# A fused attention and gated-unit kernel: a cap on the loads in flight, a different first quad, fewer paddings and another written-out order

## The chip, the cores and the metric

The kernel runs on one core of a Trainium2 chip. A core has five engines that run side by side, each with its own stream of instructions: TensorE (PE in the profile, with its weight loads as PEld), VectorE (DVE), ScalarE (ACT), GpSimd (POOL) and SyncE (SP), which here only issues DMAs. They wait for each other through semaphores. SBUF is the on-chip memory of 128 partitions; PSUM is the memory of eight banks (called B0 to B7 here) that PE writes. The metric is device time in microseconds (us) of one execution.

## The reference

Eight batches of eight heads, 576 positions, head size 64. Attention is causal by blocks of 64 positions; its output, heads side by side, is x with 512 columns. A gate is a causal convolution over five positions with one weight per tap and column, put through a sigmoid; the output is (gate * (x @ w_val)) @ w_out. Inputs and output are float32.

```python
block_i, block_j = pos[:, None] // 64, pos[None, :] // 64
scores = where(block_i >= block_j, q @ k.T / 8, -1e9)
attn = softmax(scores) @ v                        # (8, 8, 576, 64)
x = attn.transpose(0, 2, 1, 3).reshape(8, 576, 512)
gate_pre[s] = sum(conv_w[k] * x[s - 4 + k] for k in range(5))
out = (sigmoid(gate_pre) * (x @ w_val)) @ w_out
```

## The kernel before, in words

The work is cut into words, and the order of all words is written out by hand in one string, PLAN (a few more in START). `run` goes through the string and records the instructions of each word; so each engine's stream has its instructions in the order of the words. A word is a name, its indices and, after an @, the engine (A, D, P for ACT, DVE, POOL) or the PSUM banks that it uses: `cq.1.0@P` casts tensor 0 (q; 1 is k) of quad 1 on POOL.

Attention runs over 16 quads of four heads, each with two pairs of heads (pair p belongs to quad p // 2).
- `Lqk` loads q or k of a quad (576 KB) on SP's queue into one of five float32 buffers (qks), `cq` casts it to two-byte floats (qk16, three buffers), `tq` transposes it on DVE into qT or kT (two of each). In the kernel before, the cast always puts two neighbouring positions side by side (j innermost), so that the transpose can move them as one four-byte element: 576 elements a partition.
- Head r of the quad lies on partitions 32r to 32r+31 (in two chunks c), so a score matmul uses 32 rows of PE's array, and matmuls of different r use different rows. `kz` copies k's first and last block into a small tile. `s.a.t` computes one of three parts t of the score matrix for all four heads; `s.a.t.h` only for the two heads of half h. Part t = 2 needs positions from 256 on alone.
- `e` is the exponential on ACT, PSUM to pt (two-byte, six buffers), 192 in all. `m` (mask, POOL) copies block 0 to the end of pt and zeroes the masked corners.
- `Lv`, `Lvt` load v of a pair (two DMAs of 128 KB) and the tails of a batch; `cv`, `cvt` cast them on POOL. A column of ones beside v gives the sum of the weights.
- `av.p.h` multiplies weights by v (15 matmuls), `n` divides by the sum on DVE, `xtr` transposes x on PE, and `xt` brings it back to SBUF (xt).

The gated unit works in 13 units of 288 or 384 positions. `cn` is the convolution on PE: 32x32 tiles with diagonal weights (DG), 80 matmuls for a unit, or 40 for a half (`cn.n.h`, two of the four row groups); `th` is the gate's tanh on ACT, `val` the product with w_val, `gv` their product on DVE, `o` the product with w_out, `oc` its copy to one of five buffers (osb) on ACT or DVE, `st` the store on SP's queue.

Memsets ahead of PLAN and the word `pm` in it fill what never changes: ones behind pt and zeros ahead of xt. `w` are matmuls on zeros; `cw`, `cT` and `DG` make the taps' diagonals.

Quad 0 is loaded in halves (`Lqh`, `cqh`, `tqh`): each partition's first ten and last eight positions, all four DMAs on SP's queue, the word `pm` standing between their casts and `kz.0` on POOL.

In the built program, each DMA on SP's queue waits for the landing of the eighth DMA before it; loads wait besides for the cast that frees their buffer, stores for their `oc`.

Of the kernel before, what the change touches and what calls it, by code (L numbers as in the profile page):

```python
# [10 lines left out]
Lqh.0.0 Lqh.1.1  # L11
# [3 lines left out]
Lqh.0.1 cqh.0.0@D tqh.0.0 Lqh.1.0 cqh.1.0@A Lcn cqh.1.1@D cqh.0.1@P w@0 w@0 w@0 w@0 cw@0 tqh.1.1  # L15
Lvt.0 tqh.0.1 tqh.1.0 pm kz.0@P s.0.1.0@12 s.0.2@5634 Lqk.1.1 cvt.0 e.0.1.0 e.0.1.1 e.0.2.3 cT
cq.1.1@P Lqk.1.0 s.0.0.1@70 s.0.1.1@12 Lv.1 e.0.2.2 e.0.1.3 tq.1.1 e.0.0.3 e.0.0.2 kz.1@D cq.1.0@P
s.0.0.0@34 DG cv.1 tq.1.0 e.0.1.2 Lqk.2.1 e.0.0.1 m.1 e.0.0.0 s.1.1.1@07 e.0.2.1 Lqk.2.0 s.1.0.1@12
e.0.2.0 e.1.0.3 e.1.0.2 Lv.0 av.1.0@3 cq.2.1@P av.1.1@4 e.1.1.3 n.1.0 s.1.1.0@56 Lv.3 n.1.1 m.0
e.1.1.2 s.1.2.1@31 cv.0 xtr.1@2 av.0.1@4 e.1.2.3 cq.2.0@P tq.2.1 e.1.2.2 cv.3 av.0.0@0 s.1.0.0@71  # L20
e.1.1.0 Lqk.3.0 Lqk.3.1 Lv.2 m.3 kz.2@D e.1.1.1 e.1.0.1 xt.1 tq.2.0 cq.3.0@P n.0.1 n.0.0 s.1.2.0@23
s.2.2.1@56 Lv.5 e.1.0.0 e.1.2.1 Lvt.1 av.3.0@4 av.3.1@1 Lv.4 s.2.1.1@70 e.1.2.0 s.2.0.1@23 n.3.0
e.2.2.3 cq.3.1@P n.3.1 e.2.2.2 xtr.0@4 tq.3.0 e.2.1.3 cv.2 xtr.3@1 xt.0 tq.3.1 e.2.1.2 s.2.0.0@56
m.2 xt.3 e.2.0.3 s.2.1.0@40 av.2.0@7 cv.5 e.2.0.2 kz.3@D Lqk.4.1 e.2.0.0 n.2.0 e.2.0.1 cvt.1
av.2.1@1 s.2.2.0@23 e.2.1.0 m.5 s.3.2.0@56 n.2.1 cv.4 av.5.0@7 e.2.1.1 e.2.2.0 e.2.2.1 xtr.2@1
av.5.1@0 n.5.0 s.3.1.0@42 Lwv.0 e.3.2.1 cq.4.1@P Lqk.4.0 e.3.2.0 s.3.0.0@37 e.3.1.0 s.3.1.1@56
e.3.1.1 e.3.1.2 n.5.1 xt.2 xtr.5@0 m.4 e.3.1.3 tq.4.1 kz.4@D e.3.0.1 cq.4.0@P e.3.0.0 Lwv.1 xt.5
av.4.1@1 Lv.7 av.4.0@2 n.4.0 n.4.1 s.3.0.1@40 e.3.0.3 s.3.2.1@56 Lqk.5.0 m.6 cn.0.0@23 tq.4.0
e.3.0.2 e.3.2.2 e.3.2.3 wv.1@D cn.1.0@71 th.1.1 th.1.0 wv.0@D s.4.0.0@04 cv.7 s.4.1.0@56 s.4.0.1@17
m.7 th.0.1 th.0.0 e.4.1.0 cq.5.0@P val.0.1@2 av.7.0@3 e.4.1.1 Lqk.5.1 val.1.1@5 e.4.0.2 Lvt.2  # L30
e.4.0.0 val.0.0@6 gv.0.1 n.7.0 cn.0.1@23 e.4.0.1 cq.5.1@P gv.1.1 gv.0.0 tq.5.1 s.4.2@4650 e.4.0.3
th.0.3 th.0.2 s.4.1.1@17 e.4.2.1 Lv.6 e.4.2.0 wv.2@D tq.5.0 val.1.0@2 e.4.1.2 Lqk.7.0 Lvt.3 av.7.1@3
cv.6 Lqk.6.0 av.6.0@4 e.4.1.3 wv.3@P m.8 e.4.2.2 gv.1.0 av.6.1@6 n.7.1 e.4.2.3 Lv.11 s.5.2.1@21
e.5.2.3 Lqk.6.1 n.6.0 cn.1.1@73 kz.5@P e.5.2.2 n.6.1 s.5.1@4056 th.1.2 cvt.3 th.1.3 Lv.8 Lwo.2
e.5.1.1 e.5.1.2 xtr.7@1 xtr.4@2 xtr.6@3 e.5.1.0 cv.11 val.0.2@7 Lv.9 xt.7 val.1.3@1 xt.4 s.5.2.0@20
xt.6 e.5.1.3 Lv.10 e.5.2.1 e.5.2.0 gv.1.3 s.5.0@3456 e.5.0.1 e.5.0.0 cvt.2 gv.0.2 val.1.2@1 gv.1.2
val.0.3@7 cn.3.0@02 cq.6.0@P gv.0.3 tq.6.0 e.5.0.2 cq.6.1@P cv.8 Lwo.1 cn.2@4713 tq.6.1 Lwo.0
e.5.0.3 th.2.3 th.2.2 th.3.1 th.3.0 val.2.2@5 th.2.0 cq.7.0@P th.2.1 av.8.1@6 gv.2.2 m.11 val.2.3@1
# [24 lines left out]
n.19.1 av.18.0@2 o.0.8@3 s.11.1@5047 xt.16 xt.17 oc.0.8@D e.11.1.2 n.18.0 m.20 Lvt.6 cv.21
s.11.0.1@16 o.1.0@3 e.11.1.3 xtr.19@2 val.6.2@4 e.11.1.0 e.11.0.3 cv.23 Lqk.13.1 val.5.1@7 xt.19
e.11.0.2 e.11.1.1 val.5.2@2 oc.1.0@A m.21 cq.13.0@P Lv.24 s.11.2@0516 tq.12.1 gv.5.1 cv.22 e.11.2.0
gv.6.2 e.11.2.1 s.11.0.0@37 e.11.2.2 e.11.2.3 kz.12@D av.21.0@4 gv.5.2 n.21.0 av.20.1@2 xtr.18@0
val.6.0@5 e.11.0.1 xt.18 av.20.0@4 av.21.1@1 e.11.0.0 n.20.1 s.12.2@6023 m.23 gv.6.0 cv.24 n.20.0
m.22 s.12.1.0@75 Lv.26 e.12.2.3 cq.13.1@P av.23.1@4 e.12.2.2 n.21.1 e.12.2.0 cq.14.0@P tq.13.0
# [32 lines left out]
def kernel(  # L101
# [70 lines left out]
    def f32(i):  # L172
        return BK[i][0:128]
# [11 lines left out]
    def half(h):  # L185
        return (slice(0, 5), slice(5, 9))[h]

    def load_half(i, h, m):
        load_qk(0, i, m, half(h))
# [28 lines left out]
    def cast_half(i, h, m):  # L218
        cast_qk(0, i, m, half(h))
# [256 lines left out]
```

## Time and profile before

| | us |
|---|---|
| median of three runs | 189.88 (189.83 to 193.27) |
| the profiled execution | 188.78 |
| its span, first to last instruction | 186.9 |
| PE busy | 168.9 |
| DVE busy | 131.7 |
| ACT busy | 130.0 |
| POOL busy | 104.3 |

The span is what the profile's views divide; the execution's own time is 1.9 us longer. Busy is the time in which an engine had an instruction under way. In a line of the page's second part each digit is one fortieth of the span (4.67 us) and gives a share in tenths, 9 being 90% or more. The mean granted clock of PE is 0.958. DMA moved 30.42 MB in and 9.44 MB out; its packets took 70.7% of the 16 DMA engines' time.

In a line of the timeline stand the start, the duration, the engine, the line of the kernel, the operation, out<-in, partitions x elements, a count, and in brackets the idle time of the engine before it with what ended it. Line 124 is the helper that records every matmul, and line 228 the one that records every copy, so there the names of the tiles tell the step.

### The profile page before, as it was taken

The numbers are of one execution on the slowest core, as the hardware profiler recorded it, in microseconds if no ns is written. First come the engines' busy times: TensorE is split into PE (matmuls) and PEld (weight loads), VectorE is DVE, ScalarE is ACT, GpSimd is POOL, SyncE is SP. The second block draws the span as 40 slices with busy tenths as digits, with TensorE's granted clock in tenths as the row PEclk, the third lists the DMA queues.
The fourth block names the chain that finished last, engine by engine and source line by source line (L and its number), as shares of the span: only waits on it lengthen the run. The fifth ranks groups of instructions, "written<-read, shape, count | busy, mean of one in ns | idle before, by whom it ended". The sixth has DMA issues, their size and how long they took to land.

```text
span 186.9 us, 8148 instructions
## 1 busy us (share of the span) xinstructions
PE 168.9 (90%) x3433; PEld 111.0 (59%) x3433; DVE 131.7 (70%) x289; ACT 130.0 (70%) x266; POOL 104.3 (56%) x205
## 2 busy tenths in 40 slices
PE   7635999999996899899999689999999999999991
PEld 2323767776775368456667458666666668654440
DVE  6743997968695579788975588966779677832730
ACT  3393899999998187689898467698779865042342
POOL 4898899599966638788466256929074312000000
PEclk9965799999999699999999999999999999999997
DMA  6999899966999789868987999707861023003685
GB/s 202 287 347 284 226 281 383 365 203 166 238 244 402 186 226 349 208 207 221 346 215 157 262 289 297 206 4 237 257 199 61 22 95 117 4 4 112 239 308 187
DMA packets 49407, 40.39 MB, mean 216 GB/s; under 512 B 39253, under 2 KB 39509, under 8 KB 49370
## 3 DMA queue, kind: packets, MB, share of 16 engines
q1 hardware_dynamic: 49226, 39.73, 70.7%
q8 instruction: 27, 0.44, 1.1%
q10 hardware_dynamic: 144, 0.13, 0.2%
q14 instruction: 10, 0.08, 0.1%
HBM read 30.42 MB, written 9.44 MB: 213 GB/s over the span
## 4 chain that ended last, share of the span: by engine, by line
PE 65%; DVE 16%; DMA 5%; issue 5%; POOL 3%; ACT 2%; SPq 0%; ACTq 0%; DVEq 0%; POOLq 0%
PE B L124 62%; DVE kT L243 4%; PE B L310 4%; DVE qT L243 4%; DMA out_dram<-osb 3%; DVE x L303 3%; DMA qks<-in_q_dram 2%; DVE rc L302 1%; DVE xt L316 1%; DVE gv L359 1%; ACT pt L274 1%; POOL qk L228 1%; POOL pt L420 1%; ACT th L348 1%; DVE osb L228 1%
## 5 line engine op out<-in xcount | busy, mean ns | idle before, releaser
L274 ACT ACTIVATE pt<-B 128x512 f16<-128x512 f32 x192 | 98.3, 620 | 19.1 <-PE B L124 16.6
L228 POOL CAST qk<-qks 128x1152 f16<-128x1152 f32 (+1 forms) x31 | 42.3, 1377 | 5.1 <-DMA qks<-in_q_dram 3.9
L124 PE MATMUL B<-qT,kT 32*128 32x448 f16 (+3 forms) x640 | 39.5, 296 | 5.5 <-DVE qT L243 4.0
L124 PE MATMUL B<-v,pt 128*128 128x65 f16 x896 | 35.9, 195 | 2.9 <-issue 2.5
L124 PE MATMUL B<-xt,w_val 128*128 128x384 f16 (+1 forms) x208 | 37.9, 316 | 0.2 <-issue 0.2
L124 PEld LDWEIGHTS <-pt 128*128 128x128 f16 x960 | 33.8, 99 | 7.0 <-issue 4.7
L124 PE MATMUL B<-w_out,gv 128*128 128x512 f16 (+1 forms) x148 | 35.8, 380 | 2.1 <-DVE osb L228 1.1
L359 DVE SCALAR_TENSOR_TENSOR gv<-th,B 128x384 f16<-128x384 f32 (+1 forms) x52 | 26.1, 518 | 11.8 <-PE B L124 11.3
L303 DVE TENSOR_TENSOR x<-B,rc 128x320 f16<-128x320 f32 x64 | 31.5, 492 | 2.5 <-DVE rc L302 0.2
L124 PEld LDWEIGHTS <-kT 32*128 32x128 f16 x640 | 18.1, 94 | 22.2 <-issue 9.2
L348 ACT ACTIVATE th<-B 128x384 f32<-128x384 f32 (+1 forms) x52 | 20.7, 482 | 13.0 <-PE B L124 7.7
L124 PEld LDWEIGHTS <-w_val 128*128 128x128 f16 x208 | 18.3, 98 | 9.7 <-issue 1.2
L280 POOL COPY pt<-pt 64x128 f16<-64x128 f16 x32 | 10.5, 328 | 22.9 <-ACT pt L274 20.0
L124 PEld LDWEIGHTS <-gv 128*128 128x128 f16 x148 | 13.7, 99 | 15.4 <-issue 3.1
L222 POOL CAST v<-vst 128x512 f16<-128x512 f32 x32 | 19.3, 613 | 5.9 <-DMA vst<-in_v_dram 2.8
L243 DVE STREAM_TRANSPOSE kT<-qk 128x576 f32<-128x576 f32 (+2 forms) x17 | 19.7, 1156 | 4.1 <-POOL qk L228 4.1
L228 ACT COPY osb<-B 128x512 f32<-128x512 f32 (+1 forms) x18 | 10.2, 571 | 16.3 <-PE B L124 15.8
L302 DVE RECIPROCAL rc<-B 128x5 f32<-128x5 f32 x64 | 12.0, 188 | 13.5 <-PE B L124 12.0
L228 DVE COPY osb<-B 128x512 f32<-128x512 f32 x19 | 13.1, 688 | 11.2 <-PE B L124 9.0
L243 DVE STREAM_TRANSPOSE qT<-qk 128x576 f32<-128x576 f32 (+2 forms) x17 | 19.7, 1156 | 0.7 <-PE B L124 0.6
L281 POOL MEMSET pt<- 64x384 f16 x32 | 13.2, 413 | 10.3 <-ACT pt L274 8.8
L316 DVE COPY xt<-B 128x576 f16<-128x576 f16 x32 | 14.1, 450 | 4.5 <-PE B L310 4.5
(42 smaller groups left out, 123.3 us busy)
## 6 DMA issues: line engine op xcount, KB each, us to landing
out_dram<-osb SPq DMA_DIRECT2D x35, 256.0 KB, 2.9
qks<-in_k_dram SPq DMA_DIRECT2D x15, 576.0 KB, 6.7
qks<-in_q_dram SPq DMA_DIRECT2D x15, 576.0 KB, 6.9
vst<-in_v_dram SPq DMA_DIRECT2D x64, 128.0 KB, 5.2
vtst<-in_v_dram SPq DMA_DIRECT2D x8, 128.0 KB, 6.4
w_st<-in_moe_w_val_dram SPq DMA_DIRECT2D x2, 512.0 KB, 6.3
w_st<-in_moe_w_out_dram SPq DMA_DIRECT2D x4, 256.0 KB, 5.1
qks<-in_q_dram SPq DMA_DIRECT2D x1, 320.0 KB, 3.0
```

What stands on the lines that cost most here:

```text
L124: nc.tensor.matmul(out=out, lhsT=lhsT, rhs=rhs, start=start, stop=stop, skip_group_check=True)
L222: nc.gpsimd.tensor_copy(out=v16s[p % NV][0:128, 0:4, 0:2, 0:64], in_=vst[p % NVS][0:128])
L228: (eng.copy if eng is nc.scalar else eng.tensor_copy)(out=o, in_=i)
L243: nc.vector.transpose(out=(qT, kT)[i][a % NQT][0:128].bitcast(fp32).rearrange("p c (x n) -> p c n x", n=9)[:, :, n], in_=qk16[(2 * a + i) ...
L274: nc.scalar.activation(out=pts[(2 * a + r // 2) % NPT][0:128, r % 2, 512 * t:512 * t + 512], in_=f32(bank["s", a, t, r]), func=AF.Exp, bia ...
L280: nc.gpsimd.tensor_copy(out=pt[64:128, 0:2, 1536:1600], in_=pt[64:128, 0:2, 0:64])
L281: nc.gpsimd.memset(pt[64:128, 0:2, 0:1536].rearrange("p h (t s) -> p h t s", t=3)[:, :, :, 0:64], 0.0)
L302: nc.vector.reciprocal(out=rc[0:128], in_=O[:, :, 64:65])
L303: nc.vector.tensor_tensor(out=x16[p % NX16][0:128, 0:5, h, 0:64], in0=O[:, :, 0:64], in1=rc[0:128].to_broadcast([128, 5, 64]), op=ALU.mult)
L316: nc.vector.tensor_copy(out=xts[b // 2 % NX][0:128, g, b % 2, 4:4 + SEQ], in_=f16(bank["xtr", p])[:, 0:SEQ])
L348: nc.scalar.activation(out=ths[n % NTH][0:128, r, 0:w], in_=f32(bank["cn", n, r])[:, 0:w], func=AF.Tanh, bias=0.0, scale=0.5)
L359: nc.vector.scalar_tensor_tensor(out=gvs[u % 2][0:128, x, t:t + w], in0=ths[n % NTH][0:128, x, 0:w], scalar=1.0, in1=f32(bank["val", n, x] ...
```

## The change

- **Window.** Every load of q, k, v and weights goes through `load`, which makes a load wait for the landing of the third load before it (the two DMAs of a v pair count as one load). The first quad's loads, the taps and the stores are not counted.
- **First quad.** It is cut by positions instead: part 0 is 0 to 255 (eight positions on each of 32 partitions per head), part 1 is 256 to 575 (ten). k's two DMAs are issued on ACT's queue. Part 1 of both is loaded, cast and transposed first, and the first score word is t = 2. Casts: one on ACT and three on POOL, instead of one on ACT, two on DVE and one on POOL.
- **Odd quads unpaired.** In odd quads the cast is contiguous, and the transpose moves 1152 two-byte elements a partition. Even quads stay paired.
- **Score halves.** `s` can now take two halves in one word (`s.a.t.h.a.t.h@four banks`), whose matmuls are interleaved.
- **Paddings.** The mask copies all 128 partitions, so of pt only the last 64 columns are filled ahead, by six memsets on DVE; the two memsets of xt go to DVE as well. `pm` is gone; the copies of the identity matrix become the word `id`.
- **Order.** START and PLAN are written anew.

| words | before | after |
|---|---|---|
| s: whole, pair of halves, half | 27, 0, 42 | 11, 14, 46 |
| half of s followed on PE by a half of other rows | 6 | 21 |
| cn of 384: whole, half | 9, 0 | 4, 10 |
| cn of 288: whole, half | 1, 6 | 0, 8 |
| oc on ACT, on DVE | 18, 19 | 24, 13 |
| wv on ACT, DVE, POOL | 0, 3, 1 | 1, 1, 2 |
| wo on ACT, POOL | 1, 1 | 0, 2 |
| kz on DVE, POOL | 8, 8 | 11, 5 |
| w (matmuls on zeros, with those ahead of PLAN) | 13 | 9 |

```diff
@@ START, PLAN
-Lqh.0.0 Lqh.1.1
+Lqh.1.1 Lqh.0.1 Lqh.0.0 Lqh.1.0
-Lqh.0.1 cqh.0.0@D tqh.0.0 Lqh.1.0 cqh.1.0@A Lcn cqh.1.1@D cqh.0.1@P w@0 w@0 w@0 w@0 cw@0 tqh.1.1
-Lvt.0 tqh.0.1 tqh.1.0 pm kz.0@P s.0.1.0@12 s.0.2@5634 Lqk.1.1 cvt.0 e.0.1.0 e.0.1.1 e.0.2.3 cT
-cq.1.1@P Lqk.1.0 s.0.0.1@70 s.0.1.1@12 Lv.1 e.0.2.2 e.0.1.3 tq.1.1 e.0.0.3 e.0.0.2 kz.1@D cq.1.0@P
-s.0.0.0@34 DG cv.1 tq.1.0 e.0.1.2 Lqk.2.1 e.0.0.1 m.1 e.0.0.0 s.1.1.1@07 e.0.2.1 Lqk.2.0 s.1.0.1@12
...
+cqh.1.1@P Lcn id cqh.0.1@P tqh.1.1 tqh.0.1 cw@0 cqh.0.0@A cqh.1.0@P tqh.0.0 s.0.2@3412 Lqk.1.0
+e.0.2.0 Lqk.1.1 tqh.1.0 Lqk.2.1 s.0.1.0@56 e.0.2.1 cT kz.0@D cq.1.0@P e.0.2.3 e.0.2.2 Lvt.0
+s.0.1.1@70 s.0.0.1@34 Lqk.2.0 s.0.0.0@12 e.0.1.3 Lv.0 e.0.1.2 e.0.0.1 e.0.0.0 tq.1.0 cq.1.1@P
+cq.2.1@P cvt.0 tq.1.1 e.0.1.0 e.0.1.1 s.1.2.1.1.1.0@0712 tq.2.1 e.0.0.3 m.0 Lqk.3.0 e.0.0.2 kz.1@D
...
@@ -150,7 +152,7 @@
-    qk16 = ring(NQ16, [128, 9, 64, 2], fp16, "qk16")
+    qk16 = ring(NQ16, [128, 18, 64], fp16, "qk16")
...
-    def load_qk(a, i, m, n=slice(0, 9)):
-        src = (q, k)[i].rearrange("b h (p n) d -> (b h p) n d", n=18)[128 * a:128 * a + 128]
-        n = slice(2 * n.start, 2 * n.stop)
-        nc.sync.dma_start(out=qks[(2 * a + i) % NQS][0:128, n], in_=src[:, n])
-    def half(h):
-        return (slice(0, 5), slice(5, 9))[h]
-    def load_half(i, h, m):
-        load_qk(0, i, m, half(h))
+    flight = []
+    def load(key, out, in_):
+        d = nc.sync.dma_start(out=out, in_=in_)
+        if not flight or flight[-1][0] != key:
+            flight.append((key, d))
+        else:
+            flight[-1] = (key, d)
+        if len(flight) > 3:
+            tc.add_manual_dep(d.ins, flight[-4][1].ins.name,
+                              mybir.DependencyInfo(mybir.DependencyClass.Sync,
+                                                   mybir.DependencyReason.DATA), reason="window")
+    def load_qk(a, i, m):
+        src = (q, k)[i].rearrange("b h (x n) d -> (b h x) n d", n=18)[128 * a:128 * a + 128]
+        load(("qk", a, i), qks[(2 * a + i) % NQS][0:128], src)
+    PARTS = ((0, 8), (256, 10))
+    def load_part(i, h, m):
+        t, w = PARTS[h]
+        (nc.scalar if i else nc.sync).dma_start(
+            out=qks[i][0:128, 8 * h:8 * h + w].rearrange("p n d -> p (n d)"),
+            in_=(q, k)[i][0, 0:4, t:t + 32 * w].rearrange("h (x n) d -> h x (n d)", n=w))
     def load_v(p, m):
         b, g = divmod(p, 4)
         for h in range(2):
-            nc.sync.dma_start(
-                out=vst[p % NVS][0:128, 0:4, h, 0:64],
-                in_=v[b, 2 * g + h, 0:512, 0:64].rearrange("(c p) d -> p c d", p=128))
+            load(("v", p), vst[p % NVS][0:128, 0:4, h, 0:64],
+                 v[b, 2 * g + h, 0:512, 0:64].rearrange("(c p) d -> p c d", p=128))
...
-    def cast_qk(a, i, m, n=slice(0, 9)):
-        copy(m, qk16[(2 * a + i) % NQ16][0:128, n],
-             qks[(2 * a + i) % NQS][0:128].rearrange("p (n j) d -> p n d j", j=2)[:, n])
-    def cast_half(i, h, m):
-        cast_qk(0, i, m, half(h))
+    def cast_qk(a, i, m, n=slice(0, 18)):
+        o, s = qk16[(2 * a + i) % NQ16][0:128, n], qks[(2 * a + i) % NQS][0:128, n]
+        if paired(a):
+            o = o.rearrange("p (n e) d -> p n (e d)", e=2).rearrange("p n (d j) -> p n d j", j=2)
+            s = s.rearrange("p (n j) d -> p n d j", j=2)
+        copy(m, o, s)
+    def cast_part(i, h, m):
+        cast_qk(0, i, m, slice(8 * h, 8 * h + PARTS[h][1]))
...
-    def trans(a, i, m, n=slice(0, 9)):
-        nc.vector.transpose(
-            out=(qT, kT)[i][a % NQT][0:128].bitcast(fp32).rearrange("p c (x n) -> p c n x", n=9)[:, :, n],
-            in_=qk16[(2 * a + i) % NQ16][0:128, n].rearrange("p n d j -> p n (d j)").bitcast(fp32)
-            .rearrange("p n (c d) -> p c n d", c=2))
-    def trans_half(i, h, m):
-        trans(0, i, m, half(h))
+    def paired(a):
+        return a % 2 == 0
+    def trans(a, i, m, h=None):
+        t, w = (0, 18) if h is None else PARTS[h]
+        n = 8 * (h or 0)
+        o, s = (qT, kT)[i][a % NQT][0:128, :, t:t + 32 * w], qk16[(2 * a + i) % NQ16][0:128, n:n + w]
+        if paired(a):
+            o, w = o.bitcast(fp32), w // 2
+            s = s.rearrange("p (n e) d -> p n (e d)", e=2).bitcast(fp32)
+        nc.vector.transpose(out=o.rearrange("p c (x n) -> p c n x", n=w),
+                            in_=s.rearrange("p n (c d) -> p c n d", c=2))
+    def trans_part(i, h, m):
+        trans(0, i, m, h)
...
-    def scores(a, t, *x):
-        *h, m = x
-        rows = [2 * h[0], 2 * h[0] + 1] if h else range(4)
+    def steps(a, t, rows, m):
...
         for w, (o, keys, g, x, y) in enumerate(work):
             for c in range(2):
-                for r in rows:
-                    rs = slice(32 * r, 32 * r + 32)
-                    mm(f32(bank["s", a, t, r])[:, o:o + y - x], keys[rs, c, g:g + 128], qt[rs, c, x:y],
-                       start=(c == 0 and (t, w) != (0, 2)), stop=(c == 1 and (t, w) != (0, 1)))
+                yield [(f32(b)[:, o:o + y - x], keys[32 * r:32 * r + 32, c, g:g + 128],
+                        qt[32 * r:32 * r + 32, c, x:y], c == 0 and (t, w) != (0, 2), c == 1 and (t, w) != (0, 1))
+                       for r, b in zip(rows, m)]
+    def scores(*x):
+        *x, m = x
+        if len(x) == 2:
+            parts = [steps(*x, range(4), m)]
+        else:
+            parts = [steps(*x[i:i + 2], (2 * x[i + 2], 2 * x[i + 2] + 1), m[2 * i // 3:2 * i // 3 + 2])
+                     for i in range(0, len(x), 3)]
+        for group in itertools.zip_longest(*parts, fillvalue=()):
+            for w in itertools.chain(*group):
+                mm(*w)
     def exps(a, t, r, m):
         nc.scalar.activation(out=pts[(2 * a + r // 2) % NPT][0:128, r % 2, 512 * t:512 * t + 512],
@@ -277,7 +310,7 @@
     def mask(p, m):
         pt = pts[p % NPT]
-        nc.gpsimd.tensor_copy(out=pt[64:128, 0:2, 1536:1600], in_=pt[64:128, 0:2, 0:64])
+        nc.gpsimd.tensor_copy(out=pt[0:128, 0:2, 1536:1600], in_=pt[0:128, 0:2, 0:64])
         nc.gpsimd.memset(
             pt[64:128, 0:2, 0:1536].rearrange("p h (t s) -> p h t s", t=3)[:, :, :, 0:64], 0.0)
         nc.gpsimd.memset(pt[64:128, 0:2, 1344:1408], 0.0)
...
-    def pads(m):
-        for i in range(NPT):
-            nc.gpsimd.memset(pts[i][0:64, 0:2, 1536:1664], 1.0)
-            nc.gpsimd.memset(pts[i][64:128, 0:2, 1600:1664], 1.0)
-        for i in range(NX):
-            nc.gpsimd.memset(xts[i][0:128, 0:4, 0:2, 0:4], 0.0)
-    OPS["pm"] = pads
+    def idents(m):
+        nc.vector.tensor_copy(out=ident16[0:128], in_=ident[0:128])
+        for i in range(4):
+            hs = slice(32 * i, 32 * i + 32)
+            nc.vector.tensor_copy(out=idfold[hs, 0, 0:32], in_=ident[hs, 32 * i:32 * i + 32])
+    OPS["id"] = idents
     nc.vector.memset(wz[0:128], 0.0)
     run(START)
@@ -431,10 +463,10 @@
     for _ in range(9):
         warm([7])
     make_identity(nc, ident)
-    nc.vector.tensor_copy(out=ident16[0:128], in_=ident[0:128])
-    for i in range(4):
-        hs = slice(32 * i, 32 * i + 32)
-        nc.vector.tensor_copy(out=idfold[hs, 0, 0:32], in_=ident16[hs, 32 * i:32 * i + 32])
+    for i in range(NPT):
+        nc.vector.memset(pts[i][0:128, 0:2, 1600:1664], 1.0)
+    for i in range(NX):
+        nc.vector.memset(xts[i][0:128, 0:4, 0:2, 0:4], 0.0)
     for i in range(2):
         nc.gpsimd.memset(v16t[i][0:64], 0.0)
         nc.gpsimd.memset(v16t[i][64:128, 0:8, 64:65], 1.0)
```

## The prediction

> **What bounds the kernel now.** I read four views in turn: the page's 40 slices for the shape, the chain that ended last, the waits, and each engine's timeline where PE stands still.
>
> ```profile
> PE   7635999999996899899999689999999999999991
> PEclk9965799999999699999999999999999999999997
> DMA  6999899966999789868987999707861023003685
> q8 instruction: 27, 0.44, 1.1%
> ```
>
> PE is at 9 or 10 tenths from slice 4 on, and the chain is 65% PE. The weak places are the first four slices, where the granted clock falls too, and slices 13 and 22. From 15.92 us on PE is idle for 5.7 us up to its last matmul, and 4.3 us of these have one name. In the waits:
>
> ```profile
> PE B L124 <- issue: 4.3, 4, 2.5
> PE B L124 <- DVE qT L243: 4.0, 1, 4.0
> ```
>
> "issue" means that nothing the profile shows released PE. The four places are at 55, 61, 77 and 105 us; two of them, and the start of the second quad, in PE's timeline (start, duration, idle before in brackets):
>
> ```profile
> 15.92 1.78 PE L124 MATMUL B<-qT,kT 32*128 32x448 f16 x12 [4.05 <-DVE qT L243]
> ...
> 61.66 0.28 PE L124 MATMUL B<-v,pt 128*128 128x65 f16 x4 [2.47 <-issue]
> ...
> 105.39 0.59 PE L124 MATMUL B<-w_out,gv 128*128 128x512 f16 x2 [1.04 <-issue]
> ```
>
> 61.66 is inside one av, whose operands lay ready. Stretches of 1 us around it (PE, PEld, DVE, ACT, POOL busy, clock, DMA share, GB/s):
>
> ```profile
> 59.00:60.00 1.00, 0.19 (x7) 0.10 (x4) 0.00 (x0) 1.00 (x3) 1.00 (x1) 1.00 1.06 427
> ...
> 62.00:63.00 1.00, 1.00 (x9) 0.66 (x7) 0.95 (x3) 0.00 (x0) 1.00 (x2) 0.55 0.89 208
> 63.00:64.00 1.00, 1.00 (x4) 0.43 (x3) 0.77 (x3) 0.00 (x0) 0.76 (x1) 0.50 0.50 118
> ```
>
> The DMA engines are full in the gap (427 GB/s), and the clock is then halved for 3.4 us, which costs another 1.7. Queue 8 brings PE its instructions in 27 packets of 16 KB; the trace has them at 47.7, 52.8, 59.4 and 63.3 us, so the third starts inside the gap, late against its neighbours. I read the gaps as PE waiting for instructions behind loads.
>
> The start is a chain through POOL, which fills paddings between two casts (first lines), while ACT runs out of scores (last two):
>
> ```profile
> 5.04 0.71 POOL L228 CAST qk<-qks 128x512 f16<-128x512 f32 x1 [2.04 <-DMA qks<-in_q_dram]
> 5.69 0.31 POOL L420 MEMSET pt<- 64x256 f16 x1
> ...
> 9.96 0.61 POOL L225 CAST v16t<-vtst 64x512 f16<-64x512 f32 x1
> 10.64 2.74 POOL L228 CAST qk<-qks 128x1152 f16<-128x1152 f32 x2
> ```
>
> ```profile
> 8.68 6.07 ACT L274 ACTIVATE pt<-B 128x512 f16<-128x512 f32 x12 [1.53 <-PE B L124]
> 17.95 2.07 ACT L274 ACTIVATE pt<-B 128x512 f16<-128x512 f32 x4 [3.21 <-PE B L124]
> ```
>
> **Part 1, the start.** By the issue rows the four half loads take 3.0, 3.2, 3.4 and 4.2 us from their issue at 0.72, 1.17, 1.63 and 2.10, so they land at 3.7, 4.4, 5.0 and 6.3; the last 832 KB come at 326 KB/us. In the new order both 320 KB parts are issued first, on two queues: they land by 3.7 + 320/326 = 4.7, everything by 6.3. POOL casts k's part, then q's (0.71 x 640/512 = 0.89 each): 5.6, 6.5; ACT casts q's other part by 6.2; DVE transposes by 7.8. The first score word waits for q's other part too, and starts at 7.8 (8.03 before): little won. But no padding follows on POOL. Quad 1's q has landed at 6.3 + 576/326 = 8.05, its k at 9.8. Cast at 1.40: 9.5 and 11.2. Transposed at 1.22: 10.7 and 12.4. Quad 1's scores start at 12.4, not 15.92: **-3.5**. On ACT twelve exponentials take 6.07, 0.51 each; quad 0's run from about 8.5 to 14.6, and the 24th ends at 20.7 without a gap, where it now ends near 24.9 (eight at 0.51 after 20.81): -4.2. I take **-3.8**, since both engines are over 90% busy from 20 to 50 us and neither could follow alone. Ends: nothing (POOL or loads hold quads 2 and 3 back), -5.5 (PE and ACT win at every step).
>
> The paddings move to DVE: eight memsets at 0.1 (the kz memsets: 0.19 for two) end by 4.1, ahead of the first transpose at 5.6, so nothing; without that cover 0.9. The mask's copy covers 128 partitions instead of 64: 128x512 and 64x512 casts on POOL take 0.613 and 0.614, so nothing; were it double, 0.33 x 32 on POOL.
>
> **Part 2, odd quads unpaired.** Sixteen casts become contiguous: 1.40 now, and a contiguous 128x1024 cast takes 1.04, so some 1.2: 3 us of POOL, not on the path after the start. The sixteen transposes handle 1152 two-byte elements instead of 576 four-byte ones, which no row shows: 0.7 if each element were at double the present pace, 1.22 by bytes, 2.44 by elements. I take 1.22, the row with the same bytes. [...]
>
> **Part 3, PE's own work.** Score words go from 27 whole and 42 halves to 11 whole, 14 pairs and 46 halves: 69 to 71, and whole or half takes about 0.53 from start to start: +1.1. Halves of different rows that follow each other rise from 6 to 21, and such a one takes 0.38 (the trace at 37.77) instead of 0.47 to 0.53: -1.5. Conv words go from 9 whole of 384 columns, one of 288 and 6 halves of 288 to 4 whole of 384, 10 halves of 384 and 8 of 288. From start to start:
>
> ```profile
> 40.76 0.81 PE L124 MATMUL B<-xt,DG 32*32 32x288 f16 x40
> 41.50 0.80 PE L124 MATMUL B<-qT,kT 32*128 32x320 f16 x18
> ```
>
> ```profile
> 120.19 1.17 PE L124 MATMUL B<-xt,DG 32*32 32x384 f16 x80
> 121.28 0.82 PE L124 MATMUL B<-xt,w_val 128*128 128x384 f16 x4
> ```
>
> A half of 288 takes 0.74, a whole 384 takes 1.09: half the matmuls is no half of the time. A whole 288 is 0.94 (1.68 at 50.82 for a half and a whole). A half of 384, which no row shows, lies between 0.74 and 1.09; by 0.74 x 1.09/0.94 I take 0.86. Before 6 x 0.74 + 0.94 + 9 x 1.09 = 15.2; after 8 x 0.74 + 10 x 0.86 + 4 x 1.09 = 18.9: +3.7, less some 0.8 where two halves adjoin (8 times). Changes of tile shape on PE go from 93 to 100, at 0.1 (av: 0.46 before an av, 0.56 before a score): +0.7. Together **+3.0**; with both ends of the half +1 to +6. PE has no idle time to hide this.
>
> **Part 4, three loads in flight.** Now a load waits for the eighth DMA before it. A v load is two DMAs, so in flight are some 2 MB (8 x 270 KB); three loads are about 1.2 MB, at most 1.7. What stands ahead of an instruction packet falls by up to half. Of the 4.3 us I take three quarters, **-3.3** (ends: 0 and -4.3), and with the 2.47 gap goes the halved clock, **-1.7** (ends 0, -1.7). The wait stands in SP's stream: behind it are all later loads and the stores, and a late store keeps an osb buffer, for which PE now waits 1.07 once. That loads are not slowed rests on rows:
>
> ```profile
> qks<-in_k_dram SPq DMA_DIRECT2D x15, 576.0 KB, 6.7
> ...
> vst<-in_v_dram SPq DMA_DIRECT2D x64, 128.0 KB, 5.2
> ...
> qks<-in_q_dram SPq DMA_DIRECT2D x1, 320.0 KB, 3.0
> ```
>
> 6.7 and 5.2 are with eight in flight, 3.0 with nothing ahead. 1.2 MB at 326 KB/us is 3.7 us. There are 76 loads up to 139 us, or 5.5 us for three: time enough. k's first loads on ACT's queue push its table load by about 0.9, ended near 2.9, used at 8.
>
> [...]
>
> ACT takes six more output copies (18 to 24, 0.6 each) and DVE six fewer: ACT waits 16 us for PE ahead of these, so nothing; at worst 3.
>
> **Sum.** -3.8 + 3.0 - 3.3 - 1.7 = -5.8. The profiled execution took 188.78 (span 186.9); 183.0 for such a one. The median of the runs is 189.88, 1.1 higher: **184.1**, -3.1%. A measurement of this kernel can tell about 2% (3.8 us) from no change.
>
> **Rivals.**
> (a) The gaps stay, because the loads keep all DMA engines full at any depth, or the buffers held the loads to three anyway: -3.8 + 3.0 = -0.8, 189. For it: the DMA share is 9 in most slices up to 120 us. Against: PE fetches 27 blocks and stands only four times, after long bursts.
> (b) Unpaired transposes cost 2.44: quads 1, 3 and 5 add 7.3 us to DVE between 12 and 60 us, which is idle for 6.9 of 20 to 60; about half shows, 188. For: no row excludes it.
> (c) **Slower**: the window starves the casts. If three loads take over 5.5 us, loads become the bound: 0.1 us more costs 76/3 x 0.1 = 2.5 us. At 5.8 it is 7.6 - 5.8 = +1.8, with the gaps gone; at 5.9 +4.4, 194. For: landings of 5.2 to 6.9 now. Against: they are queueing, and a lone one takes 3.0.
>
> **Chances.** Forecast 0.55, (a) 0.20, (b) 0.10, (c) 0.15. The forecast's own range is 179 (-5.5 + 1 - 4.3 - 1.7 = -10.5) to 188; the whole range 179 to 193 leaves out the worse half of (c) and a little on each side. Faster by over 2% (below 186.1): most of the forecast, 0.50. Within 2%: the rest of it, (a), most of (b): 0.31. Slower: 0.19.
>
> **What would show it.** Quad 1's first scores near 12.4 and ACT without a 3.2 us gap before 20; PE's "issue" waits near 1 us and no halved clock at 62; conv halves of 384 near 0.86; unpaired transposes near 1.2; median landings of 3 to 4.5 us. I am wrong if POOL's casts wait for loads in the middle, if DVE is full up to 60 us, or if the new order makes PE wait where it did not.

## The result, and the profile after

The changed kernel takes **257.78 us** in the median (256.61 to 258.56, four runs), the kernel before in the same rounds 189.86: a ratio of 1.358, with an interval of 1.351 to 1.365. The forecast was 184.1, between 179 and 193. It missed by 74 us, and in sign. Some executions of every kernel here take some per cent longer than its others: a median is over all of them, while ratios, intervals and differences between kernels leave these out.

The page's slices of the changed kernel (its span is 254.7 us, so a slice is 6.37; they are counted from 0), with the chain that ended last:

```profile
PE   6026097897389968956999595995798499999992
DVE  3128989988958899999486779699989937662561
PEclk9655555668659988995599889897999959999999
DMA  3638879988700898439049196670707300020575
...
PE 46%; DVE 33%; issue 9%; DMA 9%; ACT 2%; SPq 1%; DVEq 0%; ACTq 0%
```

PE was at 90% or more nearly throughout before; now holes run up to slice 31, the first slices after the warming are almost empty, the clock is near 0.5 from slice 2 to 6 and again later, and DVE carries a third of the chain. DVE is busy for 190.8 us instead of 131.7. The rows of DVE's groups, shapes kept apart, tell which instruction it is (count | busy, mean ns of one | idle before):

```profile
L270 DVE STREAM_TRANSPOSE kT<-qk 128x1152 f16<-128x1152 f16 x8 | 41.2, 5151 | 0.0
L270 DVE STREAM_TRANSPOSE qT<-qk 128x1152 f16<-128x1152 f16 x8 | 41.1, 5137 | 1.6 <-PE B L126 1.6
L270 DVE STREAM_TRANSPOSE kT<-qk 128x576 f32<-128x576 f32 x7 | 8.7, 1237 | 0.0
```

An unpaired transpose moves the same bytes as a paired one and takes 5.15 us instead of 1.24. Sixteen times 3.9 is 63 us more on DVE, which had 55 us of idle time in the whole span before. The waits of PE name DVE's products:

```profile
PE B L126 <- DMA conv_nat<-in_moe_conv_w_dram: 12.5, 1, 12.5
PE B L126 <- DVE x L336: 12.4, 6, 2.8
PE B L126 <- DVE gv L392: 9.7, 5, 3.5
PE B L126 <- DVE kT L270: 7.6, 1, 7.6
```

The first line is something else: the start. POOL's timeline there shows the first casts of quad 0 waiting for its loads:

```profile
10.49 0.85 POOL L246 CAST qk<-qks 128x640 f16<-128x640 f32 x1 [7.52 <-DMA qks<-in_k_dram]
13.40 0.85 POOL L246 CAST qk<-qks 128x640 f16<-128x640 f32 x1 [2.06 <-DMA qks<-in_q_dram]
15.77 0.72 POOL L246 CAST qk<-qks 128x512 f16<-128x512 f32 x1 [1.51 <-DMA qks<-in_k_dram]
```

I had the two parts of 320 KB landed by 4.7 us and everything by 6.3. They landed at about 10.5 and 13.4, the others after 15. A window of PE's timeline gives quad 1's first scores, at 15.92 before and 12.4 in the forecast:

```profile
31.28 1.89 PE L126 MATMUL B<-qT,kT 32*128 32x320 f16 x32 [7.60 <-DVE kT L270]
```

ACT's exponentials begin at 20.28 (8.68 before), and it waits again for quad 1:

```profile
20.28 3.04 ACT L307 ACTIVATE pt<-B 128x512 f16<-128x512 f32 x6 [2.32 <-PE B L126]
...
32.35 6.23 ACT L307 ACTIVATE pt<-B 128x512 f16<-128x512 f32 x12 [5.59 <-PE B L126]
```

Why so late? The busy times from 10 to 15 us (of PE, PEld, DVE, ACT and POOL, each with its count of instructions; the last three numbers are the granted clock, the share of the 16 DMA engines that is busy, and GB/s), first of the changed kernel, then of the kernel before:

```profile
10.00:15.00 5.00, 0.00 (x0) 0.00 (x0) 1.46 (x2) 0.00 (x0) 1.70 (x2) 0.50 0.26 102
```

```profile
10.00:15.00 5.00, 1.76 (x28) 0.96 (x28) 2.90 (x4) 4.75 (x10) 4.81 (x6) 0.59 1.05 342
```

A share of 0.26 with work waiting is four engines of sixteen (0.26 x 16 = 4.2). The trace's DMA packets say the same: between 10 and 15 us four or five are under way nearly all the time on the two queues together, and 15 to 24 before. Each part's load runs over [4 heads][32][640 or 512 elements], where the old halves ran over [128 partitions]. In the trace's semaphore updates each part load lands in four steps (k's first part from 9.85 to 10.44 us), each old half in sixteen (q's first from 3.06 to 3.71). Quad 1's q, over 128 rows as well, has twelve of its sixteen by 8.2 us in the changed kernel and the last four, behind the parts, at 18.0 to 18.5. That the four heads are the reason for the four steps is so far a guess from the shapes; a run below tries it.

### The profile page after: what moved, and what is told of

Same layout as the page of the kernel before. It is cut to its first block, busy times and chain, and to the rows that moved or that the text cites. A ratio compares the mean times of both kernels' runs of the same rounds, so it can differ in the third digit from the quotient of the medians.

```text
span 254.7 us, 8160 instructions
## 1 busy us (share of the span) xinstructions
PE 195.9 (77%) x3429; PEld 129.1 (51%) x3429; DVE 190.8 (75%) x290; ACT 134.4 (53%) x272; POOL 98.8 (39%) x192
## 4 chain that ended last, share of the span: by engine, by line
PE 46%; DVE 33%; issue 9%; DMA 9%; ACT 2%; SPq 1%; DVEq 0%; ACTq 0%
PE B L126 43%; DVE kT L270 13%; DVE qT L270 10%; DMA conv_nat<-in_moe_conv_w_dram 6%; DVE gv L392 3%; PE B L343 3%; DMA out_dram<-osb 3%; DVE x L336 2%; DVE xt L349 2%; ACT pt L307 1%; DVE rc L335 1%; DVE osb L246 1%; SPq L203 1%; DVE kz L246 0%; ACT osb L246 0%
## 5 line engine op out<-in xcount | busy, mean ns | idle before, releaser
L126 PE MATMUL B<-qT,kT 32*128 32x448 f16 (+3 forms) x640 | 49.8, 344 | 28.8 <-DVE kT L270 7.6
L270 DVE STREAM_TRANSPOSE kT<-qk 128x1152 f16<-128x1152 f16 (+3 forms) x17 | 50.9, 3015 | 9.8 <-POOL qk L246 8.2
L270 DVE STREAM_TRANSPOSE qT<-qk 128x1152 f16<-128x1152 f16 (+3 forms) x17 | 51.0, 2999 | 6.7 <-ACT qk L246 3.0
L246 POOL CAST qk<-qks 128x1152 f16<-128x1152 f32 (+2 forms) x33 | 40.4, 1224 | 36.6 <-DMA qks<-in_k_dram 9.9
L126 PE MATMUL B<-v,pt 128*128 128x65 f16 x896 | 44.5, 213 | 4.8 <-DVE gv L392 3.5
L126 PEld LDWEIGHTS <-kT 32*128 32x128 f16 x640 | 23.0, 104 | 49.5 <-issue 29.5
L126 PEld LDWEIGHTS <-pt 128*128 128x128 f16 x960 | 41.9, 111 | 10.4 <-issue 7.6
L246 ACT COPY osb<-B 128x512 f32<-128x512 f32 (+1 forms) x24 | 14.0, 582 | 25.7 <-PE B L126 19.5
L335 DVE RECIPROCAL rc<-B 128x5 f32<-128x5 f32 x64 | 13.4, 209 | 16.8 <-PE B L126 11.7
L126 PEld LDWEIGHTS <-w_val 128*128 128x128 f16 x208 | 18.6, 99 | 10.9 <-issue 3.4
L126 PE MATMUL B<-xt,DG 32*32 32x384 f16 (+1 forms) x1040 | 20.8, 331 | 2.8 <-DVE x L336 2.5
L313 POOL COPY pt<-pt 128x128 f16<-128x128 f16 x32 | 9.4, 294 | 32.3 <-ACT pt L307 31.9
```

Of the source, the lines that this page charges most:

```text
L126: nc.tensor.matmul(out=out, lhsT=lhsT, rhs=rhs, start=start, stop=stop, skip_group_check=True)
L246: (eng.copy if eng is nc.scalar else eng.tensor_copy)(out=o, in_=i)
L270: nc.vector.transpose(out=o.rearrange("p c (x n) -> p c n x", n=w), in_=s.rearrange("p n (c d) -> p c n d", c=2))
L313: nc.gpsimd.tensor_copy(out=pt[0:128, 0:2, 1536:1600], in_=pt[0:128, 0:2, 0:64])
L335: nc.vector.reciprocal(out=rc[0:128], in_=O[:, :, 64:65])
```

## The experiments

**Odd quads paired again, nothing else changed.**

```diff
 def paired(a):
-    return a % 2 == 0
+    return True
```

> The changed kernel with odd quads paired again, as in the kernel before (cast interleaved, transpose of 576 four-byte elements); all else as changed. Theory A (two separate faults: 16 unpaired transposes at 5.15 instead of 1.22 us, and a first quad whose loads land 10 us late): the time falls by 14 x 3.9 = 55 for quads 3 to 15 plus 2 x 3.9 = 8 at the start, so 257.8 - 55 - 8 = 195 (193 to 203), with quad 1's first scores still about 10 us later than the 12.4 that was forecast. Rival B (the window of three loads starves the casts, or the new order is bad in itself, and DVE's longer transposes only fill time in which it would wait): the time stays above 225.

203.4 us (200.82 and 205.99), 192.0 for the kernel before on that chip. The loss falls from 68 us to 9 (200.82 against 191.9): some 59 are gone with the two-byte transposes, where 63 were expected. PE still waits 12.1 us for conv_nat.

**The same, with each part's load split into four, one per head.** Each is then a DMA of 32 rows.

```diff
-        (nc.scalar if i else nc.sync).dma_start(
-            out=qks[i][0:128, 8 * h:8 * h + w]...,
-            in_=(q, k)[i][0, 0:4, t:t + 32 * w].rearrange("h (x n) d -> h x (n d)", n=w))
+        for r in range(4):
+            (nc.scalar if i else nc.sync).dma_start(
+                out=qks[i][32 * r:32 * r + 32, 8 * h:8 * h + w]...,
+                in_=(q, k)[i][0, r, t:t + 32 * w].rearrange("(x n) d -> x (n d)", n=w))
```

> As the run with all quads paired, and besides each of the four part loads of the first quad is issued as four DMAs, one for each head (32 partitions, 32 runs in DRAM), on the same queues. Theory A: the late landing comes from the shape of the access (its slowest dimension in DRAM is 4, the heads), so all parts land by about 7 to 8 us instead of 10.5 to 17, and the whole is what the prediction priced without its two mis-sized terms: 184 (181 to 189). Rival B: above 215. Rival C (the parts are late because two queues compete, or because ACT's queue is slow): landings stay above 10 us and the time at 193 to 203.

195.47 us, 7.4 under the run before it (193.4 against 200.82); ratio to the kernel before 1.010 (0.997 to 1.024). Sixteen DMAs instead of four carry the same bytes, and the first two casts move from 10.49 and 13.40 to 5.74:

```profile
5.74 1.65 POOL L247 CAST qk<-qks 128x640 f16<-128x640 f32 x2 [2.76 <-DMA qks<-in_k_dram]
8.05 0.72 POOL L247 CAST qk<-qks 128x512 f16<-128x512 f32 x1 [0.66 <-DMA qks<-in_k_dram]
```

The last part lands at 7.9. From 0 to 5 us the DMA engines' share is 0.58 at 156 GB/s, where the run before has 0.24 at 50. So the narrow loads are shown to be the cause of the late start. The 184 that I expected of this run did not come: with both faults mended the change is still worth nothing. The start is still not that of the forecast: the first four issues on each queue stand 0.46 us apart, but each of the last four waits until an earlier part load has landed (on SP at 3.15, 3.86, 4.88 and 5.36; its waits there: 1.9 us in four), so SP and ACT are kept till 5.7 and 5.9, conv_nat is issued at 6.2, and quad 1's scores start at 15.51.

**The same without the window.**

> As the run before, with the window of three loads taken away (a load waits only for the eighth DMA before it, and for its buffer). If the prediction's part 4 is right (the window takes away most of PE's gaps on issue and one halved clock): 3 to 5 us slower than with the window, and gaps on issue of 3 to 5 us come back on PE. If the window does nothing: within 1 us. If the window costs (loads later): 1 to 5 us faster.

195.75 us, ratio 1.023 (1.009 to 1.036). The window seems to be worth about 1% here, less than the 3 to 5 us expected of part 4, and the two intervals overlap, so that it is worth anything is not shown.

**The kernel before, with the odd quads' casts and transposes unpaired, and nothing else.**

```diff
...
+        if a % 2:
+            nc.vector.transpose(out=o.rearrange("p c (x n) -> p c n x", n=18),
+                                in_=s.rearrange("p n (c d) -> p c n d", c=2))
+            return
```

> The kernel before, with only the odd quads' cast and transpose changed as in the changed kernel (cast contiguous, transpose of 1152 two-byte elements). Theory A: 16 transposes at 5.15, 63 us more on DVE, which was idle for 55 us of 187: 230 to 250. Rival B: the order before has DVE work off the path, 190 to 205.

258.32 us (255.08 and 261.57) against 192.0: +63 (255.08 against 191.9). DVE's groups:

```profile
L248 DVE STREAM_TRANSPOSE kT<-qk 128x1152 f16<-128x1152 f16 x8 | 41.0, 5122 | 3.7 <-POOL qk L231 3.7
L248 DVE STREAM_TRANSPOSE qT<-qk 128x1152 f16<-128x1152 f16 x8 | 40.9, 5112 | 0.0
```

This one edit on the old order costs nearly as much as the whole change (+63 of 68), and more than I expected: none of the 63 us finds room beside other work. How much of it comes by way of PE's clock (0.835 in the mean here, 0.93 to 0.95 in the kernel before) is not separated.

**What makes them slow: the type, or the place of the writes?** Both kinds of transpose write 36 bytes apart (18 two-byte or 9 four-byte elements). Here the two-byte ones write neighbours.

```diff
-        nc.vector.transpose(out=o.rearrange("p c (x n) -> p c n x", n=w),
+        order = "p c (x n) -> p c n x" if paired(a) else "p c (n x) -> p c n x"
+        nc.vector.transpose(out=o.rearrange(order, n=w),
```

> The changed kernel with its part loads split by head (as in the run before), odd quads still unpaired, but the sixteen odd transposes write 32 neighbouring two-byte elements at a time instead of elements 36 bytes apart; the positions inside the odd quads then come out in another order, so the arithmetic of those quads is not that of the reference, only its amount. Theory TYPE (a two-byte transpose is slow as such): 5.1 us each stays, about 247 to 258 us in all. Theory STRIDE (the two-byte writes 36 bytes apart are what costs 4.5 ns per element): each falls to between 0.7 and 2.4 us, and the time to 193 to 205 us.

194.45 us in a single execution, and the rows:

```profile
L272 DVE STREAM_TRANSPOSE qT<-qk 128x1152 f16<-128x1152 f16 x8 | 11.0, 1373 | 1.8 <-PE B L126 1.3 <-POOL qk L247 0.5
L272 DVE STREAM_TRANSPOSE kT<-qk 128x1152 f16<-128x1152 f16 x8 | 11.0, 1370 | 0.1
```

1.37 us: a two-byte transpose is not slow as such; the step between its writes makes it so. At a step of 36 bytes the width of an element counts as well: 4.47 ns for one of two bytes, 2.12 for one of four (1220 ns for 576, in the kernel before).

**How the price rises with the step.** Each odd transpose is cut into two of 576 elements with a step of its own, and the even quads' k is written side by side.

```diff
+        for c in range(2):
+            step = ((2, 6), (3, 9))[i][c]
+            nc.vector.transpose(
+                out=o[:, c].rearrange("p (l x n) -> p l n x", x=32, n=step),
+                in_=s.rearrange("p (l n) (c d) -> p c l n d", c=2, n=step)[:, c])
```

> The run with neighbouring writes again, but each odd transpose split into two of 576 two-byte elements (one for each half of the 64 columns) whose writes lie 2 or 6 elements apart (4 and 12 bytes, q) and 3 or 9 apart (6 and 18 bytes, k); the even quads' k transposes write neighbouring four-byte elements instead of elements 36 bytes apart. Positions come out in another order wherever that is so; the amount of work is the same. So far: 1.19 ns per two-byte element at a step of 2 bytes, 4.47 at 36 bytes; 2.12 per four-byte element at 36 bytes. Theory ANY GAP (a two-byte write that isn't beside the one before it is slow): all four take about 2.6 us per 576. Theory DISTANCE (the cost rises with the step): 0.8 to 1.3 us at 4 bytes, rising to 2.6 at 18 or 36. For the four-byte writes: 1.22 us if their step is free, 0.7 if it is not.

206.93 us in a single execution. In DVE's groups the first two rows hold two steps each; the third against the fourth is the four-byte pair (36 bytes apart, then neighbours):

```profile
L277 DVE STREAM_TRANSPOSE kT<-qk 128x576 f16<-128x576 f16 x16 | 29.9, 1942 | 0.0
L277 DVE STREAM_TRANSPOSE qT<-qk 128x576 f16<-128x576 f16 x16 | 22.4, 1449 | 1.3 <-PE B L126 1.3
L272 DVE STREAM_TRANSPOSE qT<-qk 128x576 f32<-128x576 f32 x7 | 8.5, 1212 | 0.0
L272 DVE STREAM_TRANSPOSE kT<-qk 128x576 f32<-128x576 f32 x7 | 5.5, 789 | 0.0
```

By single instructions, for 576 elements a partition (the ends are half of the rows with 1152):

| step between writes, bytes | 2 | 4 | 6 | 12 | 18 | 36 |
|---|---|---|---|---|---|---|
| two-byte elements, us | 0.69 | 0.83 | 1.15 | 2.07 | 2.72 | 2.57 |
| four-byte elements, us | | 0.76 | | | | 1.22 |

The theory of distance holds: the price rises up to 18 bytes (2.72 us) and doesn't rise further at 36 (2.57). Against neighbouring writes a step of 36 bytes costs 3.3 ns more for a two-byte element (4.47 - 1.19) and 0.8 for a four-byte one (2.12 - 1.32). Why these differ, and what in the memory makes the price, no run here shows.

**What is left of the change without the two faults.** Four runs take the kernel before or the new order and alter one thing. First, the kernel before with the window alone:

```diff
-        nc.sync.dma_start(out=qks[(2 * a + i) % NQS][0:128, n], in_=src[:, n])
...
+            load(("qk", a, i), qks[(2 * a + i) % NQS][0:128, n], src[:, n])
...
```

> The kernel before, its own order, with nothing but the limit of three loads in flight. The forecast's part 4 holds that the fetch gaps and the halved clock behind one go: 5.0 us less than before in the same rounds (ratio 0.974). Rival, from the run without the limit: nothing, ratio 0.995 to 1.005, with PE's issue waits still about 4 us. Rival (c) of the forecast: loads come late, ratio over 1.01.

196.89 us, ratio 1.035 (1.026 to 1.044): the window alone is a loss on the old order. PE's "issue" waits do fall, from 4.3 to 1.4 us, as the forecast's part 4 had it. But the chain that ended last goes through loads (first line; DMA was 5% before), and so do the waits of SP (second block) and of POOL (third) on DMAs:

```profile
PE 52%; DMA 21%; POOL 8%; DVE 7%; ACT 4%; issue 4%; SPq 2%; ACTq 0%; POOLq 0%; DVEq 0%
```

```profile
SPq L182 <- DMA qks<-in_q_dram: 21.4, 14, 2.7
SPq L182 <- DMA qks<-in_k_dram: 17.1, 12, 3.2
SPq L182 <- DMA vst<-in_v_dram: 10.5, 18, 2.3
```

```profile
POOL v L237 <- DMA vst<-in_v_dram: 12.9, 5, 4.7
POOL qk L243 <- DMA qks<-in_q_dram: 5.4, 5, 2.6
POOL qk L243 <- DMA qks<-in_k_dram: 4.8, 4, 2.3
```

All casts of POOL wait 26.2 us for loads, 8.7 before. A load lands sooner after its issue (k: 5.3 instead of 6.7 us) but is issued later still.

Second, the kernel before with the paddings on VectorE and the wider mask copy alone:

```diff
-Lvt.0 tqh.0.1 tqh.1.0 pm kz.0@P s.0.1.0@12 ...
+Lvt.0 tqh.0.1 tqh.1.0 kz.0@P s.0.1.0@12 ...
...
-        nc.gpsimd.tensor_copy(out=pt[64:128, 0:2, 1536:1600], in_=pt[64:128, 0:2, 0:64])
+        nc.gpsimd.tensor_copy(out=pt[0:128, 0:2, 1536:1600], in_=pt[0:128, 0:2, 0:64])
...
+    for i in range(NPT):
+        nc.vector.memset(pts[i][0:128, 0:2, 1600:1664], 1.0)
+    for i in range(NX):
+        nc.vector.memset(xts[i][0:128, 0:4, 0:2, 0:4], 0.0)
```

> The kernel before, its own order, with nothing but the paddings set by VectorE ahead of the first transpose and the mask's copy over 128 partitions. By the forecast's part 1 POOL's stretch of memsets from 5.7 to 10 us goes, so quad 1's q cast and transpose come earlier and its first scores start at 12.4 to 14 instead of 15.9: 2 to 3.8 us less, ratio 0.98 to 0.99. Rival: the start is hidden behind what follows, ratio 0.997 to 1.003, although quad 1's scores start earlier.

190.48 us, ratio 1.000 (0.994 to 1.005), and quad 1's scores start at 15.89, not a tenth earlier. POOL is free from 6.6 to 8.8 now. POOL's timeline (first line) and DVE's show what was next in line:

```profile
12.08 1.39 POOL L228 CAST qk<-qks 128x1152 f16<-128x1152 f32 x1 [0.76 <-DMA qks<-in_q_dram]
```

```profile
11.36 1.22 DVE L243 STREAM_TRANSPOSE kT<-qk 128x576 f32<-128x576 f32 x1 [2.62 <-POOL qk L228]
12.61 0.96 DVE L228 COPY kz<-kT 128x256 f16<-128x256 f16 x1
13.48 1.23 DVE L396 TENSOR_TENSOR DG<-idfold,convT 128x640 f16<-128x640 f16 x1
14.64 1.20 DVE L243 STREAM_TRANSPOSE qT<-qk 128x576 f32<-128x576 f32 x1
```

k's transpose is 0.7 earlier; q's is where it was. Its cast waits for its load and ends at 13.47 (13.38 before), so POOL gave it nothing; and from 13.48 DVE has DG under way, which the written order puts ahead of it.

Third, the new order, all paired, with the old contiguous halves of quad 0 (four loads of 128 rows on SP, the first scores after all four transposes):

```diff
...
+    def load_part(i, h, m):
+        src = (q, k)[i].rearrange("b h (x n) d -> (b h x) n d", n=18)[0:128]
+        nc.sync.dma_start(out=qks[i][0:128, half(h)], in_=src[:, half(h)])
...
-... cqh.1.0@P tqh.0.0 s.0.2@3412 Lqk.1.0
-e.0.2.0 Lqk.1.1 tqh.1.0 Lqk.2.1 s.0.1.0@56 ...
+... cqh.1.0@P tqh.0.0 tqh.1.0 s.0.2@3412 Lqk.1.0
+e.0.2.0 Lqk.1.1 Lqk.2.1 s.0.1.0@56 ...
```

> The changed order with all quads paired and with the first quad's halves loaded, cast and transposed as in the kernel before (contiguous halves of every row, four loads on SyncE; the first scores wait for all four transposes). Theory START (what is left of the loss, 2%, lies in late part loads and conv weights): first scores at about 8 to 9 us, quad 1's at 12.4 to 13.5, total 1 to 3 us under the kernel before. Theory ORDER (PE's own work in the new order is 4 us longer and the start is hidden): ratio 1.015 to 1.03, as with the parts split by head.

194.05 us, ratio 1.020 (1.010 to 1.029). The start is better than before by every mark of part 1 but the first: scores at 8.90 (8.03 before), quad 1's at 14.39, and the 24th exponential ends at 22.5 instead of 24.9. Here the forecast's chain to quad 1 came nearly true: its k is transposed by 12.70 (12.4 forecast), and what its scores then wait for is an exponential on ACT ([0.91 <-ACT pt L304]). The time is 2% longer all the same. Where it goes instead can be read from PE's stream. For every word I took the time from its first matmul to the next word's, and as its own work the median for its kind after 40 us, over the traces of ten of these kernels; what a word takes above that is counted as lost. In us, from the profiled executions:

| | own work | lost up to 10 us | 10 to 40 | after 40 |
|---|---|---|---|---|
| before | 152.0 | 7.4 | 9.6 | 13.2 |
| before with the window | 152.0 | 7.4 | 11.1 | 21.4 |
| before with the paddings moved | 152.0 | 7.4 | 11.1 | 12.4 |
| new order, paired, split by head | 156.1 | 9.8 | 11.3 | 9.4 |
| the same without the window | 156.1 | 9.3 | 15.2 | 7.6 |
| new order, paired, old halves | 156.1 | 8.7 | 14.1 | 7.0 |

The new order gives PE 4.1 us more of its own, loses 4 to 7.5 more up to 40 us and 4 to 6 less after. Up to 40 us the clock is the likely reason: with the old halves it is at 0.5 from 8.4 to 35.7 us, in the kernel before from 10.9 to 21.1. Windows of that run (PE busy, PEld, DVE, ACT, POOL, clock, DMA share, GB/s) and of the kernel before:

```profile
24.00:28.00 4.00, 4.00 (x43) 2.57 (x42) 2.49 (x5) 2.40 (x5) 2.23 (x6) 0.50 0.89 261
28.00:32.00 4.00, 4.00 (x57) 3.15 (x55) 2.22 (x6) 2.27 (x5) 3.75 (x6) 0.50 0.84 246
```

```profile
24.00:28.00 4.00, 3.91 (x82) 2.84 (x83) 3.83 (x8) 4.00 (x9) 3.75 (x8) 1.00 1.00 285
28.00:32.00 4.00, 3.75 (x86) 3.08 (x87) 3.00 (x10) 3.86 (x8) 3.75 (x9) 1.00 1.08 381
```

An av word in that run's timeline, one in the kernel before, and one in the run split by head without the window:

```profile
29.66 0.98 PE L126 MATMUL B<-v,pt 128*128 128x65 f16 x14
```

```profile
30.34 0.60 PE L124 MATMUL B<-v,pt 128*128 128x65 f16 x14
```

```profile
31.38 0.98 PE L126 MATMUL B<-v,pt 128*128 128x65 f16 x14
```

ACT, busy for 98% of these eight microseconds before, is busy for 58%, while PE has no idle time. By the last line the clock's rows seem to miss such a stretch: in that run they stand at full up to 54.9 us, though its av words take 0.93 to 0.98 us from 20 to 37.

Fourth, the four warming matmuls put back, which the new order leaves out (13 to 9), with the window and without it, and taken out of the kernel before:

```diff
-... cqh.0.1@P tqh.1.1 tqh.0.1 cw@0 ...
+... cqh.0.1@P tqh.1.1 tqh.0.1 w@0 w@0 w@0 w@0 cw@0 ...
```

> The run with all quads paired and the old halves, with one edit: the four warming matmuls that stand ahead of the taps in the kernel before, and that the new order leaves out, are put back. Its clock was halved from 8.4 to 35.7 us, that of the kernel before only from 10.9 to 21.1. Theory CLOCK (a good part of what is left comes from the long halved stretch): full clock lasts to about 11 us and returns by 21 to 25 us, and the time falls by 3 to 6 us, ratio to before 0.985 to 1.005. Theory OWN WORK (PE has 4.2 us more of its own, and ACT bounds the halved stretch): ratio stays at 1.015 to 1.03 whether or not the clock returns earlier.

> The same without the limit of three loads in flight. On the old order the limit alone cost 3.5% (PE idle 9.6 us more); on the new order, with parts split by head, its removal changed nothing or cost 1%. Theory ORDER FITS (the new order was laid out for the limit, its loads stand where the limit lets them run): ratio to before equal to or up to 2% above the run with the limit. Theory LIMIT COSTS everywhere: 2 to 4% under the run with the limit.

> The kernel before with nothing but its four warming matmuls taken out. Theory CLOCK: the halved stretch begins near 8 us and lasts beyond 25, and the time rises by 2 to 5 us, ratio 1.01 to 1.026. Rival: the warming matmuls are worth nothing here, ratio 0.995 to 1.005.

With the window 193.49 us, ratio 1.018 (1.009 to 1.027). Without it 193.74 in the median of six widely spread runs (189.08 to 195.75), where the kernel before had 192.16; no interval can be given. The kernel before without warming: 191.23, ratio 1.006 (1.000 to 1.012). The theory of the clock mostly fell: with warming the halved stretch runs from 10.6 to 31.1 instead of 8.4 to 35.7, 6.8 us less of it, and the ratio does not move (1.018 after 1.020); in the kernel before it ends at 21.9 even without warming. So that the clock causes what is left is argued from the windows and not shown. What in the new order keeps it halved some 10 us longer isn't settled, nor what the window costs there.

## Why the prediction was wrong

**Part 2 decided it.** Of the 68 us lost, some 59 go with pairing, 7.4 with the wide loads, and 1.5 stay. The step that failed is "I take 1.22, the row with the same bytes", and with it the outer bound, "2.44 by elements". 5.15 was measured. Both bounds came from rows of four-byte writes, and the row for two-byte writes 36 bytes apart did not exist. The "0.7 if each element were at double the present pace" was a slip: at half of 2.12 ns, 1152 elements come to 1.22. The 1.22 comes near the 1.37 measured with neighbouring writes, and is four times too low where they lie 36 bytes apart. Rival (b) had the right mechanism, and its place, but a price of 2.44 and half of it hidden. At 5.15 nothing is hidden, as the odd-quads run on the old order shows (+63 for 63 us of DVE). What I costed from the cast's side held: contiguous casts of 1152 take 1.15 (1.2 forecast), paired ones 1.40.

**Part 1 failed twice.** "They land by 3.7 + 320/326 = 4.7" takes a rate read where sixteen engines were busy (326 GB/s at a share of 1.08, from 4 to 6 us of the kernel before) for loads that get four (102 at 0.26): they landed at 10.5 to 13.4. Splitting them gives back 7.4 us. And "no padding follows on POOL", from which quad 1's 12.4 and the -3.8 came, named one hold of three: without paddings q's load and then DVE's DG keep the same scores at 15.89. With the new order and the old halves quad 1 starts at 14.39, held by ACT, and the exponentials are 2.4 us ahead by the 24th; but PE has lost 22.8 us by 40 us there and 17.0 before, so nothing of that is left. "eight memsets at 0.1 … so nothing" and the mask copy at nothing held (ratio 1.000).

**Part 3 held.** +3.0 was forecast (its terms add up to +3.2), 4.1 measured as PE's own work. A half of 384 takes 0.94 alone (0.86 taken) and 0.55 to 0.66 beside another; a whole one 1.10. The convolution's words come to 17.7 us with the old halves and, waits left out, 15.2 before: +2.5, forecast +2.9.

**Part 4 was right on the gaps and wrong on their price.** Where no slow transposes hold PE up, its "issue" waits are 0.4 to 2.9 us with the window (five kernels) and 3.8 to 5.6 without (five): some 3 us, as in the -3.3. Landings fell nearly as expected (3 to 4.5), here the changed kernel's DMA issues with the median from issue to landing last:

```profile
qks<-in_q_dram SPq DMA_DIRECT2D x15, 576.0 KB, 4.8
qks<-in_k_dram SPq DMA_DIRECT2D x15, 576.0 KB, 4.6
vst<-in_v_dram SPq DMA_DIRECT2D x64, 128.0 KB, 4.1
```

But the step "there are 76 loads … 5.5 us for three: time enough" is rival (c)'s door, and the kernel before with the window went through it: +3.5%, since an average hides that loads come in bursts (by slices, 157 to 402 GB/s up to 121 us of the kernel before). On the new order, what the window is worth stays open: the runs with and without it lie within each other's spread, split by head as well as with the old halves.

**The sum** of -5.8 had -3.8 and -5.0 as gains. In the new order without its two faults the loss after 40 us is indeed 4 to 6 us smaller (in the profiled executions); it pays 4.1 of own work and 4 to 7.5 up to 40 us, and ends at +1 to +2%. The forecast would have been wrong by some 8 to 10 us even with the transposes at 1.22 and all loads wide.

## What to carry to other kernels

Before an edit that changes an element's width or a pattern's order is costed, write down for both sides of each instruction and each DMA the step in bytes of the innermost write and the size of the outermost dimension; a row with the same bytes but another step (5.15 against 1.37 us) or another outer dimension (first cast at 10.49 with loads over 4 heads, at 5.74 with one over 32 rows for each head) isn't the same row. Pairing two-byte elements into one four-byte element is worth a factor of four where the writes lie 36 bytes apart (5.15 against 1.24 us). A limit on loads in flight has to be costed by its bursts: look at what the casts wait for, not at loads per microsecond.

## What the runs showed of the hardware that was not expected

- A DVE transpose of two-byte elements costs 1.19 ns an element with neighbouring writes and 4.47 with writes 36 bytes apart; of four-byte elements 1.32 and 2.12.
- A DMA over [4][32][640 or 512] floats landed in four steps, one over [128] rows in sixteen. From 10 to 15 us of the changed kernel, with those over [4] under way, the share of the DMA engines was 0.26 (four of sixteen) at 102 GB/s; in the same five microseconds of the kernel before it was 1.05 at 342 GB/s.
- TensorE's clock stayed at 0.5 while PE was busy for 4.00 of 4.00 us in one stretch after another from 20 to 35.7 us (new order, paired, old halves). In the kernel before it was back at full at 21.1, with PE busy for 4.00 of 4.00 us from 16 to 20.
- The profile's clock rows seem to miss a halved stretch: without the window they show the full clock at 31.38 us while an av word takes 0.98 us, as at 0.50 with the old halves, instead of 0.60 as at 1.00 in the kernel before.
